# GpSimd as a third engine for early softmax broadcasts and weight scalings, and floors under early due times, in a planned three-stage kernel

## The chip, the cores and the metric

The kernel runs on one core of a Trainium2 chip. The metric is device time in microseconds of one launch; the kernel before takes 798.7 us (median of 3 runs, 796.73 to 802.6). The engines are called here as the profile calls them: PE (TensorE, matrix products), PEld (its weight loads), DVE (VectorE), ACT (ScalarE), POOL (GpSimd) and SP (SyncE, which issues all DMAs).

## The reference

Three stages follow one another. `x` is 4 x 8 x 512 x 64, `state` 4 x 8 x 32 x 64. The weights arrive as 8-byte floats; all outputs are float32.

```
scores  = x @ state^T / 8;  xread = softmax(scores) @ state          # 512 rows per batch
scores2 = state @ x^T / 8;  sread = softmax(scores2) @ x             # 32 rows per batch
x = concat(xread, sread), heads merged                               # 2176 x 512
h = x @ w_in (512 x 2048); x = (h * tanh(softplus(h))) @ w_out       # "mish" layer
xn = x / rms(x) * rms_g
out = (silu(xn @ w_gate) * (xn @ w_val)) @ w_out2                    # 512 x 1536 and back
```

## The kernel before, in words

Tokens stand in five slots: slots 0 to 3 hold the 512 xread rows of batches 0 to 3, slot 4 the 128 sread rows of all batches. Every float32 product is made of three float16 products (high by high, high by low, low by high), so every weight must be turned from 8-byte floats into a high and a low float16 half on the chip.

`fetch` (L538 and on) does the first part of that for a weight piece of 512 x 512: two DMAs of 1 MB bring the raw words into one of two staging buffers (pool "raw", tile psm), and for each of four 128-row blocks k four steps follow: "hi" scales the high word to a float32 (L550, through `copy_to`, on ACT or DVE), "s" masks the sign and "l" shifts the low word (L562 on DVE, L567 on ACT or L569 on DVE), and "join" ors them together (L578, DVE only). `norms` (L599) takes sums of squares on ACT, and `pow2` (L481 on PE, then seven tiny DVE instructions, L489 to L497) makes a power-of-two scale of them. `split` writes the two halves: the high one by a scaled copy (L468 on ACT or L472 on DVE), the low one by L612 on DVE. The mish layer has four pieces each of w_in ("wi", tile w) and w_out ("wo", tile w2m), u = 0 to 3: 32 "hi" steps in all. Its pieces are called early. The nine pieces of the gated layer are converted later by `seven`, in psm and attm, and stored to DRAM ("kept", L1375), since SBUF can't hold them; they are loaded back for every slot.

`attention(b)` works off a batch in two halves g of four heads. On PE: transposes of the state (L717) and of x (L739), the scores (L752), the first softmax's product (L799), and for the second softmax transposes (L814, L838) and a product (L825), all float32. The first softmax works on 16 groups of 32 scores per partition: DVE transposes in blocks of 32 (L761), takes maxima (L770), subtracts them, broadcast over each group (L771), ACT takes the exponential (L773), DVE sums and inverts (L777 to L779), multiplies by the inverse, broadcast (L782), and transposes back (L784). The two broadcasts of 128 x 512 per half, 16 in the program, could run on DVE only. L807 on DVE writes the low half of the result into the slot.

`group(gi, c, us, ...)` multiplies slot c by some mish pieces: layer 1 (L926, 12 products of 512 columns per bank), Mish on ACT (L937), its scaled halves g (L468 or L472, and L941 on DVE), and layer 2 (L963, 6 products at a time) into four banks. Groups 0 to 5 run slots 0 and 1 through the pieces as these become ready: piece 0, then 1, then 2 and 3. Groups 6 to 8 run slots 2, 4 and 3 through all. Then the gated layer (L1111, L1195) runs slot by slot.

The order of every engine's instructions is set ahead by a planner, `Plan`. Each operation `op(engs, ...)` names the engines that may run it and its planned us on each ("T" PE, "V" DVE, "A" ACT, "G" POOL, "D" DMA). `forward` walks in planned time: a free engine takes, of the operations that are ready, the one with the smallest latest time. `late` is computed first by `chains` from due times (`at`, the planned clock of a product; T0 = 22) back along successors, and later by `backward` from the best plan; several rounds are run and the shortest plan is kept. `P.floor`, when set, gives an operation a floor: `chains` raises its latest time to it, so it stands behind anything with a smaller one. DVE has to be better by `STEAL` = 4 to take an operation that another engine may also run. The order so found is fixed in the program: each engine works its queue strictly in that order and waits where an operand isn't there yet.

## Time and profile before

| | us |
|---|---|
| median of 3 runs (lowest, highest) | 798.7 (796.73, 802.6) |
| the profiled execution | 801.31 |
| its span in the trace | 799.5 |
| granted TensorE clock, mean over the span | 0.98 of full |
| busy: PE, DVE, ACT, POOL | 772.9, 650.1, 435.8, 1.6 |

The trace covers one execution; its span leaves out 1.8 us of that execution's device time. A busy PE in it is not a PE at full clock: the granted clock of a stretch says how fast it ran. In the timeline an instruction's length includes its way through the engine's pipeline, so it may overlap the next one on the same engine. "Idle before" is what the engine waited in front of an instruction, with the instruction or DMA that released it.

### The profile page before, as it was taken

The numbers are of one execution on the slowest core, as the hardware profiler recorded it, in microseconds if no ns is written. First come the engines' busy times: TensorE is split into PE (matmuls) and PEld (weight loads), VectorE is DVE, ScalarE is ACT, GpSimd is POOL, SyncE is SP. The second block draws the span as 40 slices with busy tenths as digits, with TensorE's granted clock in tenths as the row PEclk, the third lists the DMA queues.
The fourth block names the chain that finished last, engine by engine and source line by source line (L and its number), as shares of the span: only waits on it lengthen the run. The fifth ranks groups of instructions, "written<-read, shape, count | busy, mean of one in ns | idle before, by whom it ended". The sixth has DMA issues, their size and how long they took to land.

```text
span 799.5 us, 14253 instructions
## 1 busy us (share of the span) xinstructions
PE 772.9 (97%) x5830; PEld 528.0 (66%) x5830; DVE 650.1 (81%) x1332; ACT 435.8 (55%) x802; POOL 1.6 (0%) x7
## 2 busy tenths in 40 slices
PE   7699998999999999999999999999999999999997
PEld 5344454544344444774457588888888889889996
DVE  5989999998978798897689898668975998666671
ACT  6989998854746495776366543315530744122210
POOL 0000000000000000000000000000000000000000
PEclk9689999999999999999999999999999999999999
DMA  8663733202341543605353972368353745275001
GB/s 221 190 182 99 251 97 116 73 2 105 106 155 56 213 157 156 213 15 226 157 198 145 395 275 94 137 233 283 128 217 114 275 158 185 93 294 208 2 1 66
DMA packets 36885, 125.69 MB, mean 157 GB/s; under 512 B 20052, under 2 KB 20052, under 8 KB 30676
## 3 DMA queue, kind: packets, MB, share of 16 engines
q1 hardware_dynamic: 36820, 124.79, 44.0%
q8 instruction: 45, 0.74, 0.4%
q14 instruction: 20, 0.16, 0.1%
HBM read 101.45 MB, written 23.33 MB: 156 GB/s over the span
## 4 chain that ended last, share of the span: by engine, by line
PE 71%; DVE 16%; DMA 6%; ACT 6%; issue 1%; DVEq 0%; ACTq 0%; SPq 0%
PE p L1111 25%; PE a L963 14%; PE p L926 13%; PE a L1195 12%; DMA attm<-kept_wg 3%; PE p L1271 2%; ACT junk L599 1%; DVE g L941 1%; DVE w2m L612 1%; PE a L1309 1%; DVE sxm L562 1%; DVE page L507 1%; PE a L1403 1%; DMA kept_wg<-psm 1%; ACT sxm L567 1%
## 5 line engine op out<-in xcount | busy, mean ns | idle before, releaser
L963 PE MATMUL a<-g,w2m 128*128 128x512 f16 (+1 forms) x960 | 187.1, 349 | 1.1 <-DVE slot L807 0.8
L926 PE MATMUL p<-slot,w 128*128 128x512 f16 (+1 forms) x960 | 186.8, 350 | 0.3 <-ACT tt L937 0.3
L963 PEld LDWEIGHTS <-w2m 128*128 128x128 f16 x960 | 86.0, 99 | 90.9 <-issue 5.6
L926 PEld LDWEIGHTS <-w 128*128 128x128 f16 x960 | 86.3, 99 | 90.3 <-issue 4.1
L1111 PEld LDWEIGHTS <-w 128*128 128x128 f16 x1344 | 131.3, 98 | 17.0 <-issue 0.3
L1123 DVE TENSOR_TENSOR tt<-p,tt 128x512 f32<-128x512 f32 x120 | 82.3, 688 | 31.4 <-PE p L1111 30.4
L1111 PE MATMUL p<-slot,w 128*128 128x256 f16 x768 | 93.3, 273 | 0.0
L468 ACT ACTIVATE w2m<-tt 128x512 f16<-128x512 f32 x45 | 26.9, 623 | 93.0 <-DVE tt L1162 81.1
L1111 PEld LDWEIGHTS <-attm 128*128 128x128 f16 x672 | 65.4, 98 | 10.6 <-DMA attm<-kept_wg 2.2
L1195 PE MATMUL a<-attm,w2m 128*128 128x256 f16 x576 | 66.2, 273 | 0.0
L937 ACT ACTIVATE tt<-p,page 128x512 f32<-128x512 f32 x68 | 45.8, 678 | 32.4 <-PE p L926 32.2
L1195 PEld LDWEIGHTS <-w2m 128*128 128x128 f16 x576 | 56.3, 98 | 6.7 <-issue 0.2
L941 DVE SCALAR_TENSOR_TENSOR g<-tt,page,g 128x512 f16<-128x512 f32 x68 | 50.5, 747 | 2.0 <-ACT g L468 1.3
L1195 PE MATMUL a<-psm,g 128*128 128x256 f16 x432 | 51.9, 273 | 0.0
L1111 PE MATMUL p<-slot,attm 128*128 128x256 f16 x384 | 46.2, 273 | 1.6 <-DMA attm<-kept_wg 1.3
L1195 PEld LDWEIGHTS <-g 128*128 128x128 f16 x432 | 42.2, 98 | 5.6 <-issue 0.6
L1147 ACT ACTIVATE tt<-tt,page 128x512 f32<-128x512 f32 x36 | 25.6, 719 | 35.1 <-DVE tt L1123 35.0
L468 ACT ACTIVATE psm<-psm,page 128x512 f16<-128x512 f32 (+1 forms) x39 | 27.7, 718 | 25.1 <-DVE psm L612 18.0
L1154 DVE TENSOR_TENSOR w2m<-tt,w2m 128x512 f16<-128x512 f32 x48 | 32.2, 686 | 0.9 <-ACT w2m L468 0.6
L1173 DVE TENSOR_TENSOR tt<-tt 128x512 f32<-128x512 f32 x48 | 32.2, 686 | 0.4
L567 ACT ACTIVATE sxm<-psm 128x512 uint16<-128x512 uint16 x41 | 30.9, 776 | 1.1 <-DVE w2m L578 0.6
L612 DVE SCALAR_TENSOR_TENSOR psm<-psm,page 128x512 f16<-128x512 f32 x40 | 29.9, 748 | 1.2 <-ACT psm L468 0.3
(201 smaller groups left out, 1074.2 us busy)
## 6 DMA issues: line engine op xcount, KB each, us to landing
w<-kept_wg SPq DMA_DIRECT2D x8, 1792.0 KB, 7.2
w<-kept_wv SPq DMA_DIRECT2D x8, 1792.0 KB, 7.3
attm<-kept_w SPq DMA_DIRECT2D x12, 1024.0 KB, 7.2
psm<-in_moe_w_out_dram SPq DMA_DIRECT2D x10, 1024.0 KB, 5.0
psm<-in_moe_w_in_dram SPq DMA_DIRECT2D x8, 1024.0 KB, 5.2
attm<-kept_wg SPq DMA_DIRECT2D x4, 1792.0 KB, 8.2
attm<-kept_wv SPq DMA_DIRECT2D x4, 1792.0 KB, 8.7
psm<-in_moe_w_gate_dram SPq DMA_DIRECT2D x6, 1024.0 KB, 5.0
```

What stands on the lines that cost most here:

```text
L468: nc.scalar.activation(o, i, ACTF.Copy, scale=1.0 if scale is None else scale)
L567: nc.scalar.activation(s16[:, :, 0], r16[:, :, 1], ACTF.Copy, scale=2.0 ** -13, bias=2.0 ** -14 - 0.5)
L612: op({"V": v1(512)}, lambda e: nc.vector.scalar_tensor_tensor(lo, f, s, h, ALU.mult, ALU.subtract), r=[*fn_, *hn, sname], w=ln, name=f"sl ...
L926: nc.tensor.matmul(P[ph][:, i * n:(i + 1) * n], part("wi", u, k, a)[:, f * 128:(f + 1) * 128], xh[:, k, b, :], start=m == 0, stop=m == 3 * ...
L937: op({"A": a_ps(512) + 0.09}, lambda e, s=s, ph=ph, ce=ce: nc.scalar.activation(P[s], P[ph], ACTF.Mish, scale=ce), r=[ph, f"ce{c}_{u}"], w ...
L941: op({"V": v1(512) + 0.06}, lambda e, s=s, g=g, u=u: nc.vector.scalar_tensor_tensor(P[g][:, 1, :], P[s], rho[u], P[g][:, 0, :], ALU.mult, ...
L963: nc.tensor.matmul(P[ya[d]][:, :n], part("wo", u, f, a)[:, d * 128:(d + 1) * 128], P[g][:, b, i * n:(i + 1) * n], start=first and m == 0, ...
L1111: nc.tensor.matmul(P[to][:, f * 256:f * 256 + 256], part(w, u, j, a)[:, k * 256 + f * 128:k * 256 + f * 128 + 128], h[:, k, b, :], start=b ...
L1123: op({"V": v1(512) + 0.06}, lambda e: nc.vector.tensor_tensor(P[to], P[bank_], P[a], ALU.add), r=[bank_, a], w=[to], name=f"{w} add")
L1154: op({"V": v1(512)}, lambda e: nc.vector.tensor_tensor(P[g][:, 1, :], P[s], P[g][:, 0, :], ALU.subtract), r=[s], w=[g], name="gl")
L1173: op({"V": v1(512)}, lambda e: nc.vector.tensor_tensor(P[o], P[a], P[b], f), r=[a, b], w=[o], name="gsum")
L1195: nc.tensor.matmul(P[to][:, t * 256:t * 256 + 256], P[g][:, a, o:o + 128], part("w2", u, j, b)[:, f * 256:f * 256 + 256], start=begin and ...
```

## The change

Four kinds of operation are treated differently. First, `copy_to` gets a branch for POOL, and `fetch` offers the "hi" step of pieces staged in pool "raw" (the 32 early ones) to POOL too, at a planned 0.9 us (`G1`); the planned costs of the same step on ACT and DVE rise by 0.09 and 0.06 us. Second, both broadcasts of the first softmax are offered to POOL at a planned 1.3 us (`G2`). Third, floors are set while attention 1 and wo 0 are recorded (T0 - 10), for wi and wo pieces 1, 2 and 3 (T0, T0 + 40, T0 + 80), and for attention 2 and 3 (T0 + 80 and T0 + 120). The arithmetic of every step stays as it was. The planner then finds another order for all engines.

```diff
     def copy_to(e, o, i, scale=None):
-        if e == "A":
+        if e == "G":
+            nc.gpsimd.tensor_scalar(o, i, scale, None, ALU.mult)
+        elif e == "A":
...
+    def three(early):
+
+        return {"A": a_sb(512) + 0.09, "V": v2(512) + 0.06, **({"G": G1} if early else {})}
...
-                last = op({"A": a_sb(512), "V": v2(512)}, hi, r=[r], w=dn(k), after=after, name=f"hi {w}{u}{k}")
+                last = op(three(pool == "raw"), hi, r=[r], w=dn(k), after=after, name=f"hi {w}{u}{k}")
...
-        a_op({"V": v1(512)}, lambda e: nc.vector.tensor_tensor(
+        a_op({"V": v1(512), "G": G2}, lambda e: (nc.gpsimd if e == "G" else nc.vector).tensor_tensor(
             z3(), z3(), mx.to_broadcast([128, 16, 32]), ALU.subtract), r=[zn], w=[z])
...
-        a_op({"V": v1(512)}, lambda e: nc.vector.tensor_tensor(
+        a_op({"V": v1(512), "G": G2}, lambda e: (nc.gpsimd if e == "G" else nc.vector).tensor_tensor(
             z3(), z3(), sm.to_broadcast([128, 16, 32]), ALU.mult), r=[zn], w=[z])
...
         attention(0)
         plain("wi", 0, *home["wi", 0], XEXP)
+        P.floor = lambda: T0 + -10
         attention(1)
+        P.floor = lambda: T0 + -10
         plain("wo", 0, *home["wo", 0], XEXP)
+        P.floor = None
         for u in range(1, U1):
+            P.floor = (lambda v: lambda: T0 + v)([0, 40, 80][u - 1])
             plain("wi", u, *home["wi", u], XEXP)
             plain("wo", u, *home["wo", u], XEXP)
+        P.floor = None
...
+        P.floor = lambda: T0 + 80
         attention(2, clock[0] + DUE2)
+        P.floor = None
         group(5, 1, [2, 3], 3, 1)
         flush()
+        P.floor = lambda: T0 + 120
         attention(3, clock[0] + DUE3)
+        P.floor = None
...
+G1, G2 = 0.9, 1.3
```

Line numbers of the changed kernel are higher: by 6 in `attention` (L771 becomes L777, L782 L788), in `join` (L578, L584) and `split` (L612, L618), by 2 in `copy_to` on ACT and DVE (L468, L470); "hi" on POOL is L468.

The first place is the start of DVE's queue. In the kernel before it begins, behind three memsets, with the softmax of batch 0 (tt and attm are its tiles, p_ PSUM banks, page_ small scale values):

```order
L470 COPY tt<-p_83 128x512
L470 COPY attm<-p_85 128x512
L470 COPY tt<-p_86 128x512
L761 STREAM_TRANSPOSE attm<-p_83 128x512
L770 TENSOR_REDUCE page_68<-attm 128x16
L771 TENSOR_TENSOR attm<-attm,page_68 128x512
L764 TENSOR_REDUCE page_68<-p_83 128x1
L765 TENSOR_SCALAR page_68<-page_68 128x1
L761 STREAM_TRANSPOSE attm<-p_86 128x512
L562 TENSOR_SCALAR sxm<-psm 128x512 x2
L770 TENSOR_REDUCE page_100<-attm 128x16
```

In the changed kernel the conversion of wi 0 (sxm, w_69) stands first, and the scale of the state comes before the softmax:

```order
L568 TENSOR_SCALAR sxm<-psm 128x512 x2
L575 TENSOR_SCALAR sxm<-psm 128x512
L584 SCALAR_TENSOR_TENSOR w_69<-w_69,sxm 128x512 x2
L472 COPY attm<-p_83 128x512
L472 COPY tt<-p_84 128x512
L472 COPY tt<-p_85 128x512
L494 TENSOR_SCALAR page_68<-p_86 128x4
L495 TENSOR_SCALAR page_68<-page_68 128x4
L496 TENSOR_SCALAR page_68<-page_68 128x4
L497 TENSOR_SCALAR page_68<-page_68 128x4
L498 TENSOR_SCALAR page_68<-page_68 128x4
```

The broadcasts (L771) are gone from DVE, and five conversion instructions stand ahead of the first PSUM copies.

The second place is POOL's queue from the state's memset on, which in the kernel before was its last work:

```order
masks.py:197 MEMSET ident 128x128
masks.py:199 ISA
masks.py:199 AFFINE_SELECT ident<-ident 128x128
L1410 MEMSET attm 128x1024
L1493 UNCONDITIONAL_BRANCH
```

and in the changed kernel goes on with conversions ("hi", w_69 and w2m from psm) and broadcasts (L777, L788 on attm), of which these are the first:

```order
L1416 MEMSET attm 128x1024
L468 TENSOR_SCALAR w_69<-psm 128x512 x2
L777 TENSOR_TENSOR attm<-attm,page_68 128x512
L788 TENSOR_TENSOR attm<-attm,page_68 128x512
L777 TENSOR_TENSOR attm<-attm,page_100 128x512
L468 TENSOR_SCALAR w2m<-psm 128x512 x2
L788 TENSOR_TENSOR attm<-attm,page_100 128x512
L468 TENSOR_SCALAR w2m<-psm 128x512 x2
L777 TENSOR_TENSOR attm<-attm,page_100 128x512
L788 TENSOR_TENSOR attm<-attm,page_101 128x512
L468 TENSOR_SCALAR w_69<-psm 128x512
L777 TENSOR_TENSOR attm<-attm,page_101 128x512
```

Further down the same pattern goes on to the last broadcast of batch 3: 27 conversions and 16 broadcasts in all.

The third place is PE at the transposes of batch 3 (L739, from attm into PSUM banks p_). Before, they stand behind a layer-1 product of slot 1 (slot_77) for piece 1, ahead of that group's layer 2 (L963):

```order
L926 MATMUL p_86<-slot_77,w_69 128x512
L739 MATMUL p_84<-ident,attm 128x128 x4
L739 MATMUL p_85<-ident,attm 128x128 x4
L739 MATMUL p_83<-ident,attm 128x128 x4
L739 MATMUL p_86<-ident,attm 128x128 x4
L963 LDWEIGHTS w2m
L963 MATMUL a_87<-g,w2m 128x512
```

In the changed kernel they stand (L745, with the state's transposes L723) behind a product of slot 1 for pieces 2 and 3, some 570 rows later in the queue:

```order
L932 MATMUL p_84<-slot_77,w_69 128x512
L723 MATMUL p_86<-ident,attm 128x128 x4
L745 MATMUL p_83<-ident,attm 128x128 x4
L745 MATMUL p_85<-ident,attm 128x128 x4
L745 MATMUL p_84<-ident,attm 128x128 x4
L745 MATMUL p_86<-ident,attm 128x128 x4
L969 LDWEIGHTS w2m
L969 MATMUL a_88<-g,w2m 128x512
```

The transposes moved from group 3 into group 5; the groups between them move up.

## Rows read from the trace of the kernel before

**Rows 1.** Page, part 1: each engine's busy us, share and instructions.
```profile
PE 772.9 (97%) x5830; PEld 528.0 (66%) x5830; DVE 650.1 (81%) x1332; ACT 435.8 (55%) x802; POOL 1.6 (0%) x7
```

**Rows 2.** Four stretches: busy us (instructions) of each engine, PE clock, DMA share, GB/s.
```profile
8.60:48.00 39.40, 27.78 (x160) 14.70 (x159) 36.36 (x88) 37.03 (x77) 0.00 (x0) 0.70 0.80 220
48.00:170.00 122.00, 116.57 (x738) 56.80 (x737) 117.31 (x307) 109.89 (x194) 0.00 (x0) 0.99 0.37 121
170.00:222.00 52.00, 50.14 (x228) 22.51 (x227) 46.36 (x138) 31.22 (x58) 0.00 (x0) 0.97 0.22 82
222.00:700.00 478.00, 477.00 (x3694) 343.15 (x3693) 394.15 (x713) 239.55 (x447) 0.00 (x0) 1.00 0.48 179
```

**Rows 3.** TensorE timeline: start, length, engine, line, operation; idle before and releaser.
```profile
1.05 7.06 PE L1403 MATMUL a<-ones 128*128 128x256 f16 x38 [1.05 <-DVE ones L1408]
...
48.02 2.75 PE L926 MATMUL p<-slot,w 128*128 128x512 f16 x12
...
124.51 1.09 PE L739 MATMUL p<-ident,attm 128*128 128x128 f32 x8 [1.50 <-ACT tt L937]
126.73 1.12 PE L739 MATMUL p<-ident,attm 128*128 128x128 f32 x4 [1.14 <-ACT tt L937]
...
170.16 2.75 PE L926 MATMUL p<-slot,w 128*128 128x512 f16 x12
...
213.76 0.39 PE L481 MATMUL p<-page,ones 128*128 128x8 f32 x2 [1.86 <-ACT junk L599]
```

**Rows 4.** VectorE timeline, to the last split of the first weight.
```profile
8.59 0.69 DVE L470 COPY tt<-p 128x512 f32<-128x512 f32 x1 [6.51 <-PE p L739]
...
12.83 0.69 DVE L771 TENSOR_TENSOR attm<-attm,page 128x512 f32<-128x512 f32 x1
13.44 0.68 DVE L764 TENSOR_REDUCE page<-p 128x1 f32<-128x512 f32 x1
...
46.16 0.74 DVE L612 SCALAR_TENSOR_TENSOR w<-w,page 128x512 f16<-128x512 f32 x1
```

**Rows 5.** Two short stretches behind TensorE's stops; columns as in rows 2.
```profile
124.00:132.00 8.00, 6.36 (x28) 3.24 (x28) 7.58 (x20) 5.84 (x14) 0.00 (x0) 0.79 0.30 116
...
214.00:218.00 4.00, 4.00 (x14) 1.55 (x14) 3.32 (x14) 0.95 (x2) 0.00 (x0) 0.61 0.00 0
```

**Rows 6.** Groups by line: busy us, mean ns of one, idle before; VectorE, then ScalarE.
```profile
L562 DVE TENSOR_SCALAR sxm<-psm 128x512 uint16<-128x512 uint16 x52 | 21.3, 453 | 0.5 <-DMA psm<-in_moe_w_out_dram 0.3
...
L578 DVE SCALAR_TENSOR_TENSOR w<-w,sxm 128x512 int32<-128x512 int32 x16 | 10.6, 682 | 0.1
...
L470 DVE COPY tt<-p 128x512 f32<-128x512 f32 x11 | 7.6, 688 | 17.4 <-PE p L1111 9.5 <-PE p L739 7.8
...
L771 DVE TENSOR_TENSOR attm<-attm,page 128x512 f32<-128x512 f32 x8 | 5.5, 687 | 0.1
...
L495 DVE TENSOR_SCALAR page<-page 128x1 int32<-128x1 int32 x18 | 2.8, 154 | 0.6
...
L468 ACT ACTIVATE w2m<-psm 128x512 f32<-128x512 f32 x13 | 8.5, 678 | 1.3 <-DMA psm<-in_moe_w_out_dram 1.3
```

**Rows 7.** Groups by line: GpSimd, and VectorE's clearing of the other half buffer.
```profile
L1410 POOL MEMSET attm<- 128x1024 f32 x1 | 1.0, 951 | 0.0
masks.py:199 POOL TENSOR_SCALAR_AFFINE_SELECT ident<-ident 128x128 f32<-128x128 f32 x1 | 0.3, 292 | 0.1
...
L1411 DVE MEMSET attm<- 128x1024 f32 x1 | 0.9, 912 | 0.2 <-issue 0.2
```

**Rows 8.** SyncE's DMA queue: the first weight's load, the first gated weight's store.
```profile
8.21 1.13 SPq L543 DMA_DIRECT2D psm<-in_moe_w_in_dram  x2
...
191.92 0.35 SPq L1375 DMA_DIRECT2D kept_wg<-psm  x1
```

**Rows 9.** Line 612 (splits): ns min/median/max, first and last start in us.
```profile
L612 DVE SCALAR_TENSOR_TENSOR w<-w,page x16: 740/744/754, 31.7 to 154.2; 128x512 f16<-128x512 f32 x16
L612 DVE SCALAR_TENSOR_TENSOR w2m<-w2m,page x16: 658/747/754, 56.7 to 167.1; 128x512 f16<-128x512 f32 x16
```

## The prediction

> **What bounds the kernel now.** I read the page's first part, then a table of stretches, then the TensorE timeline with its waits, then the VectorE timeline. The reader is to see first that TensorE is busy for 772.9 of 799.5 us [rows 1], so no more than about 27 us can be won by filling it. The table of stretches says where they lie [rows 2]. Between 8.6 and 48 us PE is busy for 27.78 of 39.40 us at a granted clock of 0.70. From 48 to 170 us 5.43 us are idle, from 170 to 222 us 1.86 us, and from 222 to 700 us 1.00 us of 478. The change touches only what runs before about 220 us, so it can move three things: the start of the first layer-1 product, at 48.02 us [rows 3], the idle time up to 170 us, and the stop at 213.76 us.
>
> In the two stretches from 8.6 to 170 us DVE is busy for 153.7 of 161.4 us. ACT has 146.9. What feeds PE there is DVE first of all: the last split of the first layer-1 weights begins at 46.16 us, and before it DVE works almost without a gap from 8.59 us on [rows 4]. An instruction of 0.69 us hides 0.08 us of the next, since the one at 12.83 us is followed at 13.44 us; so 512 elements cost about 0.61 us of the queue [rows 4].
>
> PE pays twice for a stop. At 124.51 and 126.73 us it waits 1.50 and 1.14 us for ACT to give a PSUM bank back [rows 3], and in the 8 us from 124 us on the granted clock is 0.79, between its levels of 1.2 and 2.4 GHz: 8 x 0.21 = 1.7 us more [rows 5]. At 213.76 us it waits 1.86 us for sums of squares of a gated weight [rows 3], and the following 4 us run at 0.61, another 1.6 us [rows 5].
>
> **The change, part by part.** Broadcasts: DVE issues 16 subtractions and multiplications fewer, 16 x 0.61 = 9.8 us of its queue (eight of them stand in [rows 6], at 687 ns). All 16 now stand on POOL. Conversions: before, ACT took 26 of the 32 (13 of them in [rows 6], at 678 ns) and DVE 6; now POOL has 27, ACT 4, DVE 1. ACT is rid of 22 x 0.67 = 14.7 us. The planner hands DVE other work for it, so DVE has only 6 instructions fewer in all, and ACT 35 fewer, although it gains two table loads. I cost those at nothing: ACT's 15 us cover their some 2.6 us. If that cover went, they would delay one Mish and so one layer-2 group by that much.
>
> POOL's prices are not in the trace. It shows a 1024-element memset of 951 ns and a select of 128 elements in 292 ns [rows 7]: 0.93 and 2.28 ns per element, so 0.48 to 1.17 us for 512 elements with one input, and to 2.34 us with two inputs read in turn. I take the numbers the change plans with, 0.9 and 1.3 us, which lie between: 27 x 0.9 + 16 x 1.3 = 45.1 us of POOL.
>
> What POOL does to DVE is not shown either. Zero is one end. The other is that every POOL instruction stops DVE for its whole length, 45.1 us; a gain is excluded, as a second engine makes no DVE instruction shorter. The nearest row is one of no stall: the two halves of one state buffer are cleared at once by POOL in 951 ns and by DVE in 912 ns [rows 7]. That is writing only, so I do not take zero but a quarter: 11 us by 220 us, 3 of them before the first product.
>
> The Trainium skill speaks against more than that. Its page "SBUF — State Buffer", section "Who interferes with whom", says that DVE and GpSimd share one port pair as an exclusive lock: a DVE instruction with two SBUF inputs, or one in a two-port fast mode, and a POOL instruction that reads SBUF shut each other out for a whole instruction. No run here shows it. Joins, splits and sign masks are of that kind, nearly half of DVE's time in this stretch, so the rule would make the estimate about 22 us instead of 11.
>
> Start. Up to the last split of the first layer-1 weight DVE had 88 instructions and now has 77. Seven broadcasts go (4.2 us), seven tiny scale instructions at 154 ns (1.1; [rows 6]), one copy and one evacuation (1.0); four PSUM copies (4 x 0.61) and one low-word shift (0.4) come: -3.5 us. The first weight load is now SP's first DMA instead of its 13th, at 8.21 us [rows 8]. So five conversion instructions (two sign masks and a low-word shift at 0.36, two joins at 0.61, by the prices of [rows 6] less the 0.08 that overlaps: 2.3 us) run before the 8.59 us at which DVE began. The price is paid by what this load passes on SP's queue: the loads of batch 0 and of the state land behind 1 MB, and DVE's first PSUM copies stand behind the conversions. PE's 38 warm-up products, which run to 8.1 us before either [rows 3], cover the state's delay. For the rest, and for the wait for the load's second half, I count 1 us. With the 3 us of stalls that makes -3.5 - 2.3 + 1 + 3 = -1.8 us, and the first layer-1 product moves as much, since the attention products that PE runs at a low clock just before it [rows 2] wait for the same queue.
>
> Gaps from 48 to 170 us. The floors move softmax 2 and 3 later: the transposes of batch 3 that waited at 124.51 us now stand some 570 PE rows further on. Counting DVE's rows in order at these prices, the last splits of wo 0, wi 1, wo 1, wi 2, wo 2, wi 3 and wo 3 come after 6.5, 2.6, 15.6, 12.8, 20.4, 4.0 and 12.2 us less work. (The same count gives 157 us for the last of before; DVE began at 8.59 us, and that split stands at 167.1 us [rows 9], so it counts rightly.) Stalls of 11 us leave all but two of these no later than before. wi 3 is 5 us later at worst (4.0 + 2.3 - 11), and its products come 15 us after its last split (154.2 us [rows 9] against the PE row at 170.16 us [rows 3]). So PE finds its weights. Of the 5.4 us of idle time and 1.7 us of slow clock I leave 1.2 us for new small waits: -5.9 us.
>
> The stop at 213.76 us. It hangs on one chain: the eighth split of the first gated weight, its store issued at 191.92 us [rows 8], the next load, ACT. That split comes 18.9 us of DVE work earlier, less 11 of stalls plus 2.3: 10 us. PE itself arrives 7.7 us earlier and with two layer-2 groups (2.6 us) fewer ahead of it. So it waits about as long; for the even chance of less I take -1.0 us out of 3.5. Beyond 222 us both kernels issue the same; nothing is counted.
>
> Sum: -1.8 - 5.9 - 1.0 = -8.7 us. The profiled execution took 801.3 us (span 799.5 and 1.8 around it); it would take 792.6. It is 2.6 us above the median of 798.7, so on the median the forecast is 790.0 us.
>
> **The rivals.** (a) POOL halts DVE: slower. Every POOL instruction stops DVE, 45.1 us in all. For: DVE has no slack up to 170 us [rows 2]. Against: the two memsets side by side [rows 7]. The place is wi 3: its cover is 4.0 + 2.3 + 15 = 21.3 us, so from stalls of 21 us on PE starves, and from 30 us on the gain of 8.7 is used up. At 37 us the kernel is 7 us slower, at 45 us 15: 806 to 814 us. By the rule that the Trainium skill gives on that page, stalls of 22 us would take about 1 us of the gain in mid-program and 3 at its start: some 794 us.
>
> (b) The stop takes it over: no change. PE comes early to the sums of squares, and the store, load and conversion behind them are paced by DMA, not by DVE; the wait of 1.86 us [rows 3] grows by what was won. Only the start's part could then be left: 797 to 800 us. For: PE's queue is in order, and that chain has some 15 us of DMA between 191.92 and 207 us. Against: its beginning is a DVE split that moves forward.
>
> (c) POOL costs DVE nothing, the other end: start -4.8, gaps -7.1, stop -3.5, together -15.4: 783 us.
>
> (d) The change does not do what it says: excluded by the order, where all 16 broadcasts and 27 conversions stand on POOL.
>
> **How the numbers follow.** A measurement of this kernel can tell about 1% (8 us) from no change. Of the cases, my forecast gets 0.45, (a) 0.20, (b) 0.20 and (c) 0.15. A result faster by over 1% is two thirds of my forecast and nearly all of (c): 0.43. Within 1% fall the rest of both and (b): 0.37. Slower by over 1% is (a): 0.20. The likeliest case is the forecast at 790 us, its own range 783 to 796. The whole range reaches from 779 (a little under c) to 808 us (the near part of a).
>
> **What would show it.** Right: the first layer-1 product near 46 us; no wait of TensorE over 1 us from 48 to 170 us and a granted clock of 1.0 there; POOL busy for 40 to 50 us with means of 0.8 to 1.2 and 1.1 to 1.6 us; joins and splits on DVE not much over 0.68 and 0.75 us. Wrong: joins or splits with means above 0.9 us, the last early split later than 167 us, or a wait of PE above 5 us at the pow2 products near 205 us. If POOL's broadcasts took over 2 us each, the softmax chain rather than DVE would set the start, and the term for it would be wrong in sign.

## The result: slower by 0.7%, and the profile after

The changed kernel takes 804.78 us (median of 7 runs, 803.41 to 805.82); the kernel before took 798.15 us beside it (7 runs). The ratio is 1.0069, 95% interval 1.0052 to 1.0086. The forecast was 790.0 us, and 0.43 on faster. The profiled execution took 804.63 us, span 802.8.

Page, part 1, of the changed kernel, where [rows 1] stood:

```profile
PE 768.9 (96%) x5830; PEld 524.5 (65%) x5830; DVE 659.4 (82%) x1326; ACT 421.6 (53%) x767; POOL 67.5 (8%) x50
```

The four stretches, where [rows 2] stood (busy us and count of PE, weight loads, DVE, ACT and POOL, then clock, DMA share, GB/s):

```profile
8.60:48.00 39.40, 25.23 (x160) 13.37 (x160) 35.80 (x86) 32.76 (x68) 21.56 (x16) 0.75 0.75 201
48.00:170.00 122.00, 112.90 (x644) 51.99 (x643) 118.32 (x304) 94.44 (x160) 37.73 (x23) 1.00 0.37 121
170.00:222.00 52.00, 50.92 (x312) 24.95 (x311) 44.52 (x114) 33.37 (x63) 4.63 (x4) 1.00 0.22 82
222.00:700.00 478.00, 475.97 (x3675) 341.21 (x3672) 399.23 (x731) 240.38 (x447) 0.00 (x0) 1.00 0.48 179
```

From 48 to 170 us PE is now idle for 9.10 us, against 5.43. From 8.6 to 48 us it is 14.17 against 11.62, from 170 to 222 us 1.08 against 1.86, and from 222 to 700 us 2.03 against 1.00. Over the span PE is idle 7.3 us more and, at a mean granted clock of 0.987 instead of 0.980, busy 4.0 us less. ACT is rid of 15 us from 48 to 170 us, as counted. DVE is as busy as before, although 16 broadcasts have left it: over the whole span it has 6 instructions fewer and 9.3 us more.

TensorE's timeline (columns as in [rows 3]; L932 is L926 of before, L969 is L963, L745 is L739, L483 is L481, L1117 is L1111):

```profile
46.90 3.71 PE L932 MATMUL p<-slot,w 128*128 128x512 f16 x12
...
123.55 2.75 PE L932 MATMUL p<-slot,w 128*128 128x512 f16 x12
126.80 2.75 PE L932 MATMUL p<-slot,w 128*128 128x512 f16 x12 [0.51 <-ACT tt L943]
131.78 4.06 PE L969 MATMUL a<-g,w2m 128*128 128x512 f16 x18 [2.23 <-DVE slot L986]
136.59 1.46 PE L969 MATMUL a<-g,w2m 128*128 128x512 f16 x6 [0.75 <-DVE slot L986]
...
144.33 0.66 PE L745 MATMUL p<-ident,attm 128*128 128x128 f32 x4 [1.50 <-ACT tt L943]
...
384.95 0.39 PE L483 MATMUL p<-page,ones 128*128 128x8 f32 x2 [1.48 <-ACT junk L605]
...
414.97 1.25 PE L1117 MATMUL p<-slot,w 128*128 128x256 f16 x10
```

The old stops at 124.51, 126.73 and 213.76 us are gone. In their place stand waits for evacuations (L986), for a bank that ACT gives back (L943), and one at 384.95 us for sums of squares. The first gated product is at 414.97 us. In the kernel before it reads:

```profile
411.12 1.15 PE L1111 MATMUL p<-slot,w 128*128 128x256 f16 x9
```

So the change is 3.85 us behind there, and 3.3 us at the end of the span: all is lost before the gated layer's own products. (The medians lie 6.6 us apart; the profiled execution of before, 801.31 us, was 3.2 us above the median of its 7 runs, that of after at its own.)

Groups by line: GpSimd over the span, then VectorE from 8.6 to 170 us (busy us, mean ns):

```profile
L468 POOL TENSOR_SCALAR w2m<-psm 128x512 f32<-128x512 f32 x15 | 26.2, 1767 | 17.5 <-DMA psm<-in_moe_w_out_dram 17.5
L468 POOL TENSOR_SCALAR w<-psm 128x512 f32<-128x512 f32 x12 | 20.6, 1734 | 19.4 <-DMA psm<-in_moe_w_in_dram 19.4
L777 POOL TENSOR_TENSOR attm<-attm,page 128x512 f32<-128x512 f32 x8 | 10.3, 1291 | 86.6 <-DVE page L776 46.2 <-PE p L932 40.4
L788 POOL TENSOR_TENSOR attm<-attm,page 128x512 f32<-128x512 f32 x8 | 9.0, 1122 | 30.4 <-DVE page L785 20.4 <-ACT attm L470 5.7 <-ACT junk L605 3.3
```

```profile
L568 DVE TENSOR_SCALAR sxm<-psm 128x512 uint16<-128x512 uint16 x36 | 19.4, 561 | 0.5 <-DMA psm<-in_moe_w_gate_dram 0.4
L947 DVE SCALAR_TENSOR_TENSOR g<-tt,page,g 128x512 f16<-128x512 f32 x20 | 17.1, 853 | 0.4
L584 DVE SCALAR_TENSOR_TENSOR w2m<-w2m,sxm 128x512 int32<-128x512 int32 x16 | 11.9, 763 | 0.3
L584 DVE SCALAR_TENSOR_TENSOR w<-w,sxm 128x512 int32<-128x512 int32 x15 | 11.4, 771 | 0.9 <-POOL w L468 0.5
```

A conversion on POOL takes 1.75 us where the planner counts 0.9. Beside POOL, sign masks (L568) take 108 ns more than the 453 of [rows 6], joins (L584) 83 and 89 ns more.

### The profile page after: what moved, and what is told of

Its sections match the earlier page's. It is cut to its first block, busy times and chain, and to the rows that moved or that the text cites. A ratio compares the mean times of both kernels' runs of the same rounds, so it can differ in the third digit from the quotient of the medians.

```text
span 802.8 us, 14301 instructions
## 1 busy us (share of the span) xinstructions
PE 768.9 (96%) x5830; PEld 524.5 (65%) x5830; DVE 659.4 (82%) x1326; ACT 421.6 (53%) x767; POOL 67.5 (8%) x50
## 4 chain that ended last, share of the span: by engine, by line
PE 59%; DVE 27%; DMA 6%; ACT 5%; issue 2%; POOL 0%; SPq 0%; DVEq 0%; ACTq 0%; POOLq 0%
PE p L1117 26%; PE a L1201 13%; PE a L969 9%; PE p L932 7%; DVE g L947 3%; DMA attm<-kept_wg 2%; DVE sxm L568 2%; DMA kept_wg<-psm 2%; PE p L1277 2%; DVE w2m L618 2%; DVE psm L618 1%; ACT junk L605 1%; DVE attm L618 1%; DVE w L584 1%; DVE w L618 1%
## 5 line engine op out<-in xcount | busy, mean ns | idle before, releaser
L969 PE MATMUL a<-g,w2m 128*128 128x512 f16 (+1 forms) x960 | 187.5, 347 | 3.5 <-DVE slot L986 3.0
L932 PE MATMUL p<-slot,w 128*128 128x512 f16 (+1 forms) x960 | 185.5, 348 | 2.0 <-ACT tt L943 1.3
L932 PEld LDWEIGHTS <-w 128*128 128x128 f16 x960 | 86.3, 99 | 93.9 <-issue 6.1
L969 PEld LDWEIGHTS <-w2m 128*128 128x128 f16 x960 | 85.4, 99 | 92.2 <-issue 6.9
L1117 PEld LDWEIGHTS <-w 128*128 128x128 f16 x1344 | 131.4, 98 | 17.2 <-issue 0.2
L1117 PE MATMUL p<-slot,w 128*128 128x256 f16 x768 | 93.4, 273 | 0.0
L1117 PEld LDWEIGHTS <-attm 128*128 128x128 f16 x672 | 65.5, 98 | 10.8 <-DMA attm<-kept_wg 1.6
L470 ACT ACTIVATE w2m<-tt 128x512 f16<-128x512 f32 x43 | 25.8, 623 | 85.7 <-DVE tt L1168 75.2
L943 ACT ACTIVATE tt<-p,page 128x512 f32<-128x512 f32 x68 | 45.8, 678 | 27.1 <-PE p L932 26.9
L947 DVE SCALAR_TENSOR_TENSOR g<-tt,page,g 128x512 f16<-128x512 f32 x68 | 53.3, 786 | 1.3 <-ACT g L470 0.2
L1117 PE MATMUL p<-slot,attm 128*128 128x256 f16 x384 | 46.0, 273 | 1.2 <-DMA attm<-kept_wg 1.0
L573 ACT ACTIVATE sxm<-psm 128x512 uint16<-128x512 uint16 x46 | 34.6, 776 | 8.8 <-DVE w L584 5.3
L470 ACT ACTIVATE psm<-psm,page 128x512 f16<-128x512 f32 (+1 forms) x35 | 24.8, 719 | 26.1 <-DVE psm L618 19.6
```

Source lines behind the costliest of these rows:

```text
L470: nc.scalar.activation(o, i, ACTF.Copy, scale=1.0 if scale is None else scale)
L573: nc.scalar.activation(s16[:, :, 0], r16[:, :, 1], ACTF.Copy, scale=2.0 ** -13, bias=2.0 ** -14 - 0.5)
L932: nc.tensor.matmul(P[ph][:, i * n:(i + 1) * n], part("wi", u, k, a)[:, f * 128:(f + 1) * 128], xh[:, k, b, :], start=m == 0, stop=m == 3 * ...
L943: op({"A": a_ps(512) + 0.09}, lambda e, s=s, ph=ph, ce=ce: nc.scalar.activation(P[s], P[ph], ACTF.Mish, scale=ce), r=[ph, f"ce{c}_{u}"], w ...
L947: op({"V": v1(512) + 0.06}, lambda e, s=s, g=g, u=u: nc.vector.scalar_tensor_tensor(P[g][:, 1, :], P[s], rho[u], P[g][:, 0, :], ALU.mult, ...
L969: nc.tensor.matmul(P[ya[d]][:, :n], part("wo", u, f, a)[:, d * 128:(d + 1) * 128], P[g][:, b, i * n:(i + 1) * n], start=first and m == 0, ...
```

## The experiments

**The theories.** First theory: POOL is the loss. Either it takes time from DVE (stalls), or its conversions come out late. Second theory: the order is the loss, since the floors and the new costs make the planner write every queue anew, and POOL is nearly free. The kernel before ran again beside each group of versions, with medians from 798.15 to 800.47 us. Differences between versions are given below as those of their medians; by the ratios some come out smaller, by up to 1.3 us. All runs:

```
version                                          median us   ratio to before, 95%
the change                                         804.78    1.0069  1.0052-1.0086
floors, raised costs, no POOL ("floors only")      798.66    0.9996  0.9980-1.0011
POOL only, no floors                               816.78    1.0212  1.0187-1.0238
broadcasts on POOL, floors                         815.98    1.0201  1.0178-1.0223
conversions on POOL, floors                        804.87    1.0062  1.0043-1.0082
the change, planner told 1.75 and 1.2              805.25    1.0061  1.0038-1.0084
order of the change, conversions as memsets        800.67    1.0016  1.0003-1.0030
order of the change, memset + spare scaling        802.02    1.0026  1.0015-1.0036
order of the change, POOL reads neighbours         803.97    1.0059  1.0038-1.0080
order of the change, conversions on DVE            806.84    1.0085  1.0070-1.0101
order of the change, conversions on ACT            807.35    1.0091  1.0076-1.0107
order of the change, all on DVE, POOL idle         809.84    1.0120  1.0104-1.0137
order of floors only, POOL busy at the start       802.16    1.0036  1.0019-1.0053
order of floors only, POOL busy throughout         806.08    1.0077  1.0064-1.0091
raised costs alone, no POOL, no floors             805.41    1.0079  1.0054-1.0103
floors, broadcasts on POOL, old costs              802.96    1.0037  1.0023-1.0050
floors, late conversions on POOL                   804.92    1.0056  1.0043-1.0069
floors at old costs, no POOL                       806.43    1.0082  1.0063-1.0101
floors under softmax 3 and 4 only, old costs       809.12    1.0118  1.0097-1.0139
```

**One half of the change each.** The floors without POOL (the raised costs of ACT and DVE stay):

```diff
-                last = op(three(pool == "raw"), hi, ...
+                last = op(three(False), hi, ...
-        a_op({"V": v1(512), "G": G2}, lambda e: ...
+        a_op({"V": v1(512)}, lambda e: ...
... (the same for the other broadcast)
```

> The change with its floors and its costs kept, POOL offered nothing (first conversions on ACT or DVE, both broadcasts on DVE). First theory (POOL is the loss: its conversion takes 1.75 us where the planner counts 0.9, and DVE's copies and joins beside it are 0.08 to 0.11 us longer each): the loss is gone, 796 to 800 us, the time of the kernel before, and DVE's L568 is back at 453 ns. Second theory (the floors and the order that comes of them are the loss, POOL is nearly free): 803 to 808 us, as the changed kernel's 804.8 or worse by the 45 us of DVE and ACT work that POOL no longer carries.

798.66 us, the time of the kernel before: here the second theory falls in its simple form, since the floors and raised costs without POOL lose nothing. POOL without the floors:

```diff
-        P.floor = lambda: T0 + -10
...
-            P.floor = (lambda v: lambda: T0 + v)([0, 40, 80][u - 1])
...
-        P.floor = lambda: T0 + 80
...
-        P.floor = lambda: T0 + 120
```

> The change without its floors: POOL is offered both kinds of work, every piece keeps its own latest time. First theory (POOL is the loss): as slow as the changed kernel or slower, 803 to 808 us. Second theory (the floors are the loss): 790 to 798 us, faster than the kernel before by part of the 8.7 us that the sum had.

816.78 us, slower than either theory said. Each half of POOL's work, with the floors; of the two edits of the floors-only version, the first of these takes the second alone, and the other the first alone:

> The floors and the conversions on POOL, both broadcasts back on DVE. By either form of the first theory: 802 to 806 us, as the changed kernel. If the broadcasts are what hurts: 797 to 801 us.

> The floors and the 16 broadcasts on POOL (1.05 to 1.4 us each, as planned), no conversion there. By either form of the first theory the 27 conversions are two thirds of POOL's time and of the loss: 797 to 801 us. If the broadcasts are what hurts (they stand in the chain from the first softmax to the product that waits for it): 803 us or more.

Without the broadcasts the time is that of the change, 804.87 us. With the broadcasts alone it is 815.98 us: less on POOL and 11 us slower, which POOL's occupation cannot explain.

**Raised costs alone.** In the traces of the two slow versions PE is busy for only 281 and 282 of the 289 us from 411 to 700 us, where POOL does nothing. Both have the loads and stores of the gated layer in another order on SP. The planner writes that order also for a version without POOL and floors, from the raised costs alone:

```diff
-                last = op({"A": a_sb(512), "V": v2(512)}, hi, ...
+                last = op({"A": a_sb(512) + 0.09, "V": v2(512) + 0.06}, hi, ...
```

> No POOL, no floors: of the change only the raised planned costs of a conversion (0.09 us on ACT, 0.06 on DVE). The planner gives the gated part of this version the same late order of loads as in the two versions that took 816 us. If that order costs the 9 to 11 us that their traces lose after the first gated product: 805 to 812 us although POOL is idle. If POOL was the cause there: 797 to 801 us.

805.41 us, with POOL idle. The stretch from 411 to 700 us, first in this version, then in the changed kernel, and PE's waits of this version from 408 us on (total us, times, longest):

```profile
411.00:700.00 289.00, 282.42 (x2472) 239.21 (x2470) 234.90 (x402) 120.69 (x197) 0.00 (x0) 1.00 0.52 192
```

```profile
411.00:700.00 289.00, 288.45 (x2521) 244.54 (x2518) 238.07 (x410) 125.64 (x211) 0.00 (x0) 1.00 0.54 198
```

```profile
PE p L1117 <- DVE tt L1129: 3.0, 4, 1.2
PE p L1117 <- DMA w<-kept_wg: 1.8, 1, 1.8
PE a L1201 <- DVE g L1160: 1.4, 3, 0.7
```

The 6 us that are gone stand in the gated layer: 6.58 us idle there against 0.55. Changes of 0.09 and 0.06 us in planned costs do this by order alone. The two versions at 816 us have that order too, and are 11 us slower than the others with POOL; 6 to 7 of the 11 stand in this stretch.

**POOL busy for nobody.** To see what POOL takes without any new order, the floors-only version got scalings of a spare tile that nothing waits for; every other engine's order stays as it was. First 27 of them in a row from the start:

```diff
+                if pool == "raw" and (w, u, k) not in DROP:
+                    op({"G": 1.75}, lambda e: nc.gpsimd.tensor_scalar(spare, spare, 1.0, None, ALU.mult), after=[last])
```

> The version with the floors alone (798.7 us), every engine's order as it stands there, and POOL given 27 scalings of a spare tile of 128 x 512 that nobody reads, back to back from about 8.6 us. Only what POOL takes from others is left: no operation waits for POOL. If the loss of the changed kernel is DVE's stalls beside POOL: L568 rises from 452 ns to 550 or more while POOL runs (8.6 to some 55 us), DVE ends that stretch 8 to 11 us of work later, and the time is 802 to 806 us. If the loss is that conversions come out of POOL late (1.75 us for a planned 0.9), this kernel stays at 797 to 800 us.

802.16 us, 3.5 us more than the floors alone. Then 32, each behind the join of a tile, of which POOL reads one column first:

```diff
+                    def burn(e, k=k):
+                        nc.gpsimd.tensor_scalar(spare[:, :1], dst(k)[:, 0, :1], 1.0, None, ALU.mult)
+                        nc.gpsimd.tensor_scalar(spare, spare, 1.0, None, ALU.mult)
```

> The version with floors alone (798.7 us), every engine's order as there; POOL reads one column of each joined tile and then scales a spare tile of 128 x 512, 32 times, so its some 51 us are spread from about 14 to 115 us and not crowded before 48. If what POOL takes from DVE in mid-program comes through to the end, as the drift between 60 and 117 us says: 803 to 808 us, with L568 and L947 near 560 and 850 ns. If only the start counts: 799 to 802 us.

806.08 us, 7.4 us more than the floors alone (6.5 by the ratios), the clearest run of the study. The single columns take 14.2 us, so POOL is busy for 71.6 us in all, a little more than the 67.5 of the change. Its groups (GpSimd, then VectorE from 8.6 to 170 us), then the same two VectorE groups with POOL idle:

```profile
L594 POOL TENSOR_SCALAR spare<-spare 128x512 f32<-128x512 f32 x32 | 55.4, 1731 | 2.6
```

```profile
L570 DVE TENSOR_SCALAR sxm<-psm 128x512 uint16<-128x512 uint16 x36 | 17.7, 516 | 1.5 <-DMA psm<-in_moe_w_gate_dram 1.4
L954 DVE SCALAR_TENSOR_TENSOR g<-tt,page,g 128x512 f16<-128x512 f32 x20 | 15.2, 769 | 0.4
```

```profile
L947 DVE SCALAR_TENSOR_TENSOR g<-tt,page,g 128x512 f16<-128x512 f32 x22 | 16.3, 748 | 0.4
L568 DVE TENSOR_SCALAR sxm<-psm 128x512 uint16<-128x512 uint16 x36 | 15.4, 452 | 0.6 <-DMA psm<-in_moe_w_gate_dram 0.6
```

So POOL's mere work slows DVE, and DVE's lateness comes through to the end: the stalls are shown, with no conversion late: no engine waits for a spare scaling here. The means rose less than I expected (516 and 769 ns, not 560 and 850), the time as much.

**The order of the change, with POOL's conversions made short.** The emitted instruction alone is exchanged:

```diff
-            nc.gpsimd.tensor_scalar(o, i, scale, None, ALU.mult)
+            nc.gpsimd.memset(o, 0.0)
```

> The changed kernel in its own order, with POOL's 27 conversions replaced by a memset of the same tile, so the converted weights' leading words are left out. It takes 27 x 1.75 = 47 us of POOL down to some 15 and reads nothing. First theory (POOL's time and what it takes from DVE): DVE's L568 falls from 561 ns toward 453, L947 from 853 toward 745, the losses between 48 and 233 us fall from 15.1 to 12.4 us or less, and the time is 798 to 801 us. Second theory (the order alone): 803 to 806 us, although POOL's work is short.

800.67 us: 4.1 us of the loss are gone. TensorE's timeline, where the changed kernel waits 2.23 us at 131.78 us; the memset version in the same rows of the program:

```profile
122.33 5.34 PE L932 MATMUL p<-slot,w 128*128 128x512 f16 x24
127.51 5.41 PE L969 MATMUL a<-g,w2m 128*128 128x512 f16 x24
```

VectorE's timeline, the g-half and the evacuations that this product waits for, in the changed kernel and then in the memset version:

```profile
130.31 0.75 DVE L947 SCALAR_TENSOR_TENSOR g<-tt,page,g 128x512 f16<-128x512 f32 x1
130.98 1.40 DVE L986 SCALAR_TENSOR_TENSOR slot<-a,page,slot 128x512 f32<-128x512 f32 x2
```

```profile
125.19 0.75 DVE L947 SCALAR_TENSOR_TENSOR g<-tt,page,g 128x512 f16<-128x512 f32 x1
125.86 1.40 DVE L986 SCALAR_TENSOR_TENSOR slot<-a,page,slot 128x512 f32<-128x512 f32 x2
```

DVE issues the same instructions in both and comes 5.1 us earlier to the evacuation; PE comes 1.2 us earlier (122.33 against 123.55 us) and waits no more. Between 60 and 117 us POOL is busy for 31.2 us in the one and 7.5 in the other, and it is there that DVE's lead grows, from 0.6 us at its 119th instruction to 5.6 at its 230th. Two caveats. POOL isn't free here: the sign masks (L568) still take 515 ns and the g-halves (L947) 782. And a memset reads nothing, so it waits for no load either. The next version was to part DVE's time from late conversions:

```diff
-            nc.gpsimd.tensor_scalar(o, i, scale, None, ALU.mult)
+            nc.gpsimd.memset(o, 0.0)
+            nc.gpsimd.tensor_scalar(spare[:, :352], spare[:, :352], 1.0, None, ALU.mult)
```

> The changed kernel in its own order; POOL's conversion becomes a memset of the tile (0.58 us; the conversion itself is left out) followed by a scaling of 352 columns of a spare tile, some 1.1 us, that nobody waits for. POOL is as busy as in the changed kernel and DVE beside it as much disturbed, but the tile is ready 1.1 us earlier. If late conversions are the loss: 800 to 802 us, as with the memset alone (800.7). If DVE's stalls are: 803 to 806 us.

802.02 us lies between the two forecasts, and the run doesn't part them: the memsets ran ahead of the loads, so POOL worked at other times than in the changed kernel (8.3 instead of 16.4 us from 60 to 90 us).

Then POOL's conversion with another input (the conversion itself is left out), and the whole change with other planned costs:

```diff
+                    if e == "G":
+                        a = raw()[:, j, 0:512].rearrange("p (a f) -> p a f", a=2)
```

> The changed kernel in its own order, POOL's 27 conversions reading 512 neighbouring words instead of every second one (whole numbers times zero, so the conversion itself is left out). If the step of 8 bytes is what makes one 1.75 us, one falls to 0.9 to 1.0 us, the planner's price, and the time lies with that of the memset version: 799 to 803 us by the first theory, 803 to 806 by the second. If not, one stays at 1.5 to 1.8 us and nothing moves by more than 1 us.

One conversion still takes 1.68 and 1.69 us and the time is 803.97 us, 0.8 us less. The step of 8 bytes isn't what makes it long.

```diff
-G1, G2 = 0.9, 1.3
+G1, G2 = 1.75, 1.2
```

> The change with the planner told POOL's measured times: 1.75 for a conversion instead of 0.9, 1.2 for a broadcast instead of 1.3; POOL is still given 27 conversions. If late conversions are the loss, the planner now orders joins and copies by the true times and 797 to 801 us come out. If DVE's stalls are the loss, they stay (27 x 1.75 us on POOL), and the time stays at 802 to 806 us.

POOL is given 27 again, and 805.25 us come out. A planner that knows POOL's own times, but not what they do to DVE, gains nothing. In the changed kernel itself the waits for POOL's conversions are few; of VectorE and ScalarE these are all (total us, times, longest):

```profile
DVE w L584 <- POOL w L468: 0.5, 1, 0.5
```

```profile
ACT junk L689 <- POOL w L468: 0.8, 1, 0.8
```

So of the two forms of the first theory the late conversion is the small one: 1.3 us, and no product waits for it directly.

**The order of the change, with POOL's work handed back in place.**

```diff
-            nc.gpsimd.tensor_scalar(o, i, scale, None, ALU.mult)
+            nc.vector.tensor_scalar(o, i, scale, None, ALU.mult)
```

(on ACT `nc.scalar.activation(o, i, ACTF.Copy, scale=scale)` stands there; in the third version the broadcasts too go to `nc.vector`)

> The changed kernel in its own order, with POOL's 27 conversions issued to DVE at their places (0.42 us each, 11.3 us more DVE work); the broadcasts stay on POOL. If what POOL takes from DVE is nearly what it carries for it (8 to 9 us of stalls beside the conversions), the time moves little: 803 to 808 us. If conversions that come late are the loss, they now come 1.3 us sooner: 798 to 801 us.

> The changed kernel in its own order, with POOL's 27 conversions issued to ACT at their places (0.68 us each, 18 us more on an engine that is idle for 28 of the 122 us from 48 to 170); the broadcasts stay on POOL. DVE loses the stalls beside the conversions (8 us or so) and gains no work. By stalls: 797 to 801 us, at or below the kernel before. If the order of the change is itself bad: 803 us or more.

> The changed kernel in its own order with POOL idle: 27 conversions and 16 broadcasts issued to DVE at their places (27 x 0.42 + 16 x 0.69 = 22.4 us more work, 11 to 12 us of stalls gone). By stalls: DVE's net load grows by 11 us on a stretch in which it is 97% busy, 806 to 812 us. By late results from POOL: 797 to 801 us.

806.84 us with the conversions on DVE, 807.35 with them on ACT, 809.84 with both kinds on DVE. So in this order POOL helps: it carries 22.4 us of DVE work (27 x 0.42 + 16 x 0.69), takes 11 us back, and the 11 us that remain are worth 5 (4 by the ratios). The version with all on DVE takes 11 us more than the floors-only one (10 by the ratios), and POOL is idle in both. The stretch from 48 to 170 us, first in the former, then in the latter, whose profiled execution, 795.95 us, lies 2.7 us below its median:

```profile
48.00:170.00 122.00, 113.44 (x643) 51.71 (x640) 117.91 (x331) 95.86 (x162) 0.00 (x0) 0.99 0.37 121
```

```profile
48.00:170.00 122.00, 119.11 (x681) 55.56 (x680) 117.69 (x317) 99.25 (x174) 0.00 (x0) 1.00 0.38 121
```

PE is idle for 8.56 us in the one and 2.89 in the other. DVE is equally full in both, but a full engine doesn't show how much it still has to do. That is seen by counting up to one and the same instruction, the first evacuation of layer 2 (L986). The stretch ahead of it in the version with all on DVE, in the floors-only version and in the changed kernel:

```profile
0.00:132.71 132.71, 112.73 (x624) 55.45 (x624) 122.38 (x314) 102.03 (x177) 1.60 (x7) 0.90 0.56 169
```

```profile
0.00:119.74 119.74, 103.11 (x598) 51.60 (x599) 109.43 (x278) 104.92 (x188) 1.59 (x7) 0.94 0.59 179
```

```profile
0.00:130.97 130.97, 110.75 (x624) 54.10 (x624) 119.62 (x277) 101.92 (x177) 60.39 (x44) 0.92 0.57 171
```

The version with all on DVE has 36 DVE instructions and 12.95 us of DVE work more ahead of it than the floors-only one, and reaches it 12.97 us later. So DVE's load explains this difference, and it is no sign of a worse order. The changed kernel has as many DVE instructions ahead of it as the floors-only one (277 and 278), with eight broadcasts fewer among them: the planner has filled their place with other work. They take 10.2 us longer, and the evacuation begins 11.2 us later. Summed with each at the mean of its kind in the version with all on DVE, where POOL is idle, they would take 125.3 us, and those of the floors-only version took 125.2: the 10 us are POOL's stalls.

For ACT I had expected a gain. Its table of busy time hid that its queue too is in order: from 8.6 to 170 us DVE waits there 2.6 us for low-word shifts of ACT and 2.5 us for its scaled copies.

**Searching for a version that beats both.** Four more edits of the change, each a choice of its parts: floors and broadcasts at the old costs; floors with conversions of later pieces only; floors alone at the old costs; of these floors the last two alone.

```diff
-        return {"A": a_sb(512) + 0.09, "V": v2(512) + 0.06, **({"G": G1} if early else {})}
+        return {"A": a_sb(512), "V": v2(512), **({"G": G1} if early else {})}
...
-                last = op(three(pool == "raw"), hi, ...
+                last = op(three(pool == "raw" and u >= 2), hi, ...
```

> The floors and the 16 broadcasts on POOL, no conversion there, the conversions at the old planned costs; the gated part has the order of the changed kernel. POOL is busy for some 19 us and DVE is rid of 9.8 us. If the 816 us of the version with broadcasts alone came from its gated order for 9 to 11 us: 803 to 807 us remain. If broadcasts on POOL are a gain by themselves: 794 to 798 us. If they alone cost 17 us: 812 or more.

> The floors; only the conversions of the third and fourth pieces are offered to POOL (it gets 12 of them, some 21 us), the broadcasts are on DVE. By stalls: 12 x 1.75 x 0.2 = 4 us taken from DVE against 12 x 0.61 or so given to DVE and ACT: 798 to 803 us. As a gain: 794 to 797 us.

> All floors, no POOL, the conversions at the old planned costs. Against the floors with the raised costs (798.7 us) it shows how far a new plan alone moves the time, and against the broadcasts on POOL at the old costs (803.0) what those cost: 797 to 800 us if POOL costs them 3 to 6 us; 802 to 804 if that was the plan.

> Only the floors under the third and fourth softmax, no POOL, old planned costs. The two waits for a bank at 124.51 and 126.73 us of the kernel before should go, as the softmax moves later: 795 to 798 us if these waits were worth their 2.6 us and 1.7 us of slow clock; 798 to 801 if other waits take their place; 805 or more if the gated part gets the slower order.

None does: 802.96, 804.92, 806.43 and 809.12 us; the second and third are slower than anything I had expected of them. The third is the sharpest lesson: it differs from the floors-only version by 0.09 and 0.06 us in planned costs and is 7.8 us slower (6.9 by the ratios) with POOL idle in both. PE's waits from 48 to 415 us in it:

```profile
PE p L483 <- ACT junk L605: 6.1, 4, 2.6
PE p L932 <- DVE page L491: 2.8, 1, 2.8
```

Four stops at sums of squares of gated weights, of the kind that stands once between 222 and 411 us in the changed kernel, at 384.95 us. The five plans that were run with POOL idle (before; floors only; raised costs; floors at old costs; late floors) run from 798 to 809 us.

## Why the prediction was wrong

**The stalls were sized rightly, by luck.** The forecast took 11 us of DVE. The excess over [rows 6] and over the same groups of before is 36 x 108 ns (L568), 20 x 108 (L947, 745 ns before), 16 x 83 and 15 x 89 (L584), 16 x 96 (L618 to w2m, 838 against 742) and 12 x 40 (L474 to g, 523 against 483): 3.9 + 2.2 + 1.3 + 1.3 + 1.5 + 0.5 = 10.7 us. The size came out by two errors that cancel: POOL works 67 us, not 45.1, since a conversion takes 1.75 us and not 0.9, and DVE loses a sixth of that, not a quarter. The rule of the Trainium skill ("SBUF — State Buffer", section "Who interferes with whom") holds in kind. A sign mask that normally takes 0.45 us stands for 1.32 us beside a broadcast on POOL. VectorE's timeline, then GpSimd's:

```profile
121.41 1.32 DVE L568 TENSOR_SCALAR sxm<-psm 128x512 uint16<-128x512 uint16 x1
```

```profile
121.07 1.34 POOL L788 TENSOR_TENSOR attm<-attm,page 128x512 f32<-128x512 f32 x1 [8.68 <-DVE page L785]
```

DVE's ends 0.3 us after POOL's, so it stood until POOL's was through, as that page says; evacuations and reductions, which it exempts, stayed at 742 and 675 to 679 ns. The estimate of 22 us made from it was twice too high.

**The start came nearly as forecast and was worth nothing.** The first layer-1 product came at 46.90 us (forecast 46.2; 48.02 before). But the first 12 ran in 3.71 us instead of 2.75 ([rows 3] and above), at a granted clock of 0.50 up to 48.8 us, and only 40 transposes of x stood ahead of them where 44 had stood before, so four were still to do. That gave all of it back.

**The step that failed** is the term for the gaps from 48 to 170 us: "So PE finds its weights. Of the 5.4 us of idle time and 1.7 us of slow clock I leave 1.2 us for new small waits: -5.9 us." Its premise held. The last splits, line 618 of the changed kernel:

```profile
L618 DVE SCALAR_TENSOR_TENSOR w<-w,page x16: 659/744/751, 25.0 to 158.3; 128x512 f16<-128x512 f32 x16
L618 DVE SCALAR_TENSOR_TENSOR w2m<-w2m,page x16: 737/742/1606, 47.8 to 162.6; 128x512 f16<-128x512 f32 x16
```

wi 3 is 4.1 us later than in [rows 9] (counted: 5), wo 3 is 4.5 us earlier (counted: 12.2 + 2.3 - 11 = 3.5). No product waited for a weight in mid-program. But PE waited for other things in the same two queues: evacuations of layer 2 (2.23 and 0.75 us), ACT's Mish (1.50, 0.77 and 0.51), scales (0.70), copies of the attention (0.86, 0.67, 0.49). The idle time is 9.1 us where 1.2 was left, 7.9 too much; of the term only the slow clock came true, 1.00 instead of 0.99. I counted DVE's queue up to the splits alone and took the 11 us of stalls as covered there. The evacuations have no such cover. The first of layer 2 (L986, L980 before) begins at 130.98 us against 130.10, while PE has issued 336 layer products by then against 294, so PE waits for it. In the order of the change the memset version begins it 5.1 us earlier and has 4.04 us of idle time there instead of 9.10:

```profile
48.00:170.00 122.00, 117.96 (x667) 54.40 (x665) 117.88 (x322) 96.34 (x162) 14.87 (x22) 0.98 0.36 121
```

None of the forecast's signs of being wrong came: no join or split has a mean above 0.9 us, the last early split began at 162.6 us, and no pow2 product waited for 5 us. What failed is a sign of being right, that no wait be over 1 us.

**Smaller steps.** The stop at 213.76 us is gone, its 1.86 us and the slow clock behind it, where -1.0 was counted. The store on its chain was issued at 184.07 us, 7.9 us earlier than in [rows 8] (counted: 10), and the same products, now at 214.03 us, wait for nothing; the 0.62 us at 216.25 us are for the scale of slot 4 (L859). SyncE's queue, then TensorE's timeline:

```profile
184.07 0.36 SPq L1381 DMA_DIRECT2D kept_wg<-psm  x1
```

```profile
214.03 0.28 PE L483 MATMUL p<-page,ones 128*128 128x8 f32 x2
...
216.25 0.38 PE L483 MATMUL p<-page,ones 128*128 128x1 f32 x2 [0.62 <-ACT junk L859]
```

"Beyond 222 us both kernels issue the same; nothing is counted" was wrong: the late gated weight at 384.95 us costs 1.48 us, and idle time from 222 to 700 us is 2.03 us against 1.00.

**The rivals.** None of them describes it. (a) gave the right sign, yet stalls are far from its 37 us and PE doesn't starve for weights. (b) was not put to the test, since PE came to these products at 214.03 us and no earlier than before (211.90, where its wait began). (c) is the nearest to the memset version, which takes 800.67 us, not 783; but 5.9 of the 10.7 us of longer instructions are left in it. The floors-only version has no stalls, as many DVE instructions ahead of the first evacuation as the change, and takes 798.66 us. That is the heart of it: even with DVE undisturbed a plan with these floors gains nothing. The change takes 6 us more. In its own order 4.1 us go when POOL's conversions become short; that the rest are the stalls that are left is likely, but not shown. What was missing was a rival for the plan itself, that every queue is written anew, that the planner fills DVE again, and that other instructions become late. Plans with POOL idle spread over some 10 us (798.7 to 809.1), more than the whole forecast gain of 8.7.

**What stays open.** Why the planner's orders differ so much in time isn't settled; the versions that reorder show that they do, not which of its rules makes it. Nor is it settled why the floors-only version, with its first evacuation 10 us earlier than before, ends no sooner. How far the memset's 4.1 us come from loads that no longer wait for POOL's reading (2.1 us of waits on SP's queue in the changed kernel) isn't parted. And the stops that the forecast summed were read from one execution, 3.2 us above the median of seven: whether each of them stands in a usual one can't be read from it.

## What to carry to other kernels

Where a planner writes the order, change the engine of an instruction in place first, with every queue kept: that prices the engine. Here POOL cost 6 to 7 us when its work was for nobody, and was worth 4 to 5 us where it stood for work of DVE; the new plan lost 6.6 us all the same, since the planner had filled DVE again. When counting a shared in-order queue, count to everything that another engine waits for, evacuations and small scales too, and not only to the pieces that the change is about. A second engine that reads SBUF beside a VectorE that is 97% busy is not free: of each microsecond of GpSimd some 0.16 us came back as longer VectorE instructions in the change, and 0.11 in both spare versions (VectorE's busy time 660.8 and 663.4 us against 656.0, for 43 and 70 us more of GpSimd).

## What the runs showed of the hardware

A one-input scaling of 128 x 512 floats took POOL 1.59 us back to back on a spare tile, 1.68 us from neighbouring whole words and 1.75 us with a step of 8 bytes, all beside a busy DVE; the shortest took 1.49, 1.48 and 1.51 us. That is longer than a two-input broadcast of the same size (1.12 and 1.29 us), and nearly three times the memset of 0.58 to 0.60 us. I had expected one input to be the cheaper case.
